# Attention scores as three float32r products of split queries and keys, in a fused attention and feed-forward kernel

## The chip, the core and the metric

The kernel runs on one core of a Trainium2 chip. The core has five engines that work beside each other, each in the order of its own queue: TensorE (PE, matrix products), VectorE (DVE), ScalarE (ACT), GpSimd (POOL) and SyncE (SP, which here only issues transfers). They meet through semaphores. Products land in PSUM, eight banks of 2 KB a partition; all else lives in SBUF, 128 partitions. The metric is the device time of one execution in microseconds, lower being better.

## What is computed

```python
def _attn_ref(q, k, v, tau):                 # (8, 8, 576, 64): batch, heads, positions, width
    scores = matmul(q, k.transpose(0, 1, 3, 2)) / sqrt(64)
    thresh = max(scores, axis=-1, keepdims=True) - tau
    scores = where(scores >= thresh, scores, -1e9)
    scores = scores - max(scores, axis=-1, keepdims=True)
    attn = exp(scores)
    attn = attn / (sum(attn, axis=-1, keepdims=True) + 1e-9)
    return matmul(attn, v)

def _moe_ref(x, w_in, w_out, a, b):          # x: (4608, 512); w_in: (512, 2048)
    h = x @ w_in
    P = a[0] + a[1] * h + a[2] * h**2 + a[3] * h**3
    Q = 1.0 + abs(b[0]) * abs(h) + abs(b[1]) * h**2
    return (P / (Q + 1e-6)) @ w_out
```

The threshold lies only tau = 0.02 below the largest score of a row, so a score that is a little off can fall on the other side of it. That is why the scores are computed to nearly full float32.

## The kernel before

**Tiling.** Heads go in pairs, 4 pairs in each of 8 batches, so 32 pairs. The 576 positions of a pair are cut into four tiles of 128 and a remainder of 64; the remainders of the pair's two heads are put together into one tile. A *unit* is one tile of one pair: 128 full units (two heads each) and 32 remainders. Units are grouped in 56 *visits*, seven a batch: three pairs are visited twice, first for tiles 0 and 1, later for tiles 2, 3 and the remainder, and the fourth pair once, for all of them. Each visit loads the queries that it needs and the keys of its pair.

**A unit.** `f_qk` computes the scores of 128 queries with all 576 keys in float32, each head on its own 64 rows of the array, in a 512-wide and a 64-wide product, into three banks (line 810; line 800 for a remainder). DVE takes the row maximum (818), ACT or DVE the threshold (825, 827), ACT cuts (833) and exponentiates with the sum (837), ACT or DVE the reciprocal's input (842, 844), then the weights are split into two f16 parts (`hi` at 347 or 349, the rest at 859), transposed by DMA from SP (869) and multiplied with the values on PE (928). In the first batch the weights are transposed on PE instead (882, 887) and multiplied in float32 (912).

**The feed-forward part.** It runs in steps of 512 hidden columns for 256 positions: the first layer in three f16 products of parts (1045), the rational function on DVE and ACT (1054 to 1087), the result split in two float32r parts (339 or 341, 1095), the second layer in three float32r products (1104). The weights come as pairs of words; ACT and DVE rebuild the float from them early in the program (`decode_ops`: `f1` 506, `f2` 509, `f4` 513, `f6` 354).

**What sets the order.** The code records operations with engine, duration, sort key, what they follow and which buffers they take and drop. `Plan.order` then walks through a model of the engines and puts each operation into the queue of an engine; operations with two engines in their price table (`FLEX`) go where they would end sooner, weighed by `EARLY` and `PRICE`. `TURN` and `KIND` are tables of numbers that shift the sort keys by place and by kind of operation. An engine's queue runs strictly in the order so made. Where the model sees PE idle in the first 400 us it puts in small products whose result nobody reads (`f_warm`, line 1248).

**The names that the change touches.** `QQs` and `KKs` are two buffers each for queries and keys, float32, loaded from SP by `ldq` and `ldk` inside `load_ops` (lines 643 to 663). `f_qk` reads them directly. In `decode_ops`, `f2` shifts the low words on ACT, and `ld` makes GpSimd wait for an older weight load by a one-element operation (498) where loads would crowd.

Of the kernel before, what the change touches and what calls it, by code (L numbers as in the profile page):

```python
# [46 lines left out]
NQ = 2  # L47
# [93 lines left out]
class Plan:  # L141
# [51 lines left out]
    def order(self):  # L193
# [1097 lines left out]
```

## Time and profile before

| | us |
|---|---|
| median of 2 runs | 1269.24 (1267.21 to 1271.28) |
| the profiled execution | 1266.8 |
| its span, first to last instruction | 1265.0 |
| granted TensorE clock, mean | 0.991 |
| score products on PE (lines 810 and 800), busy | 175.5 + 38.8 |
| second-layer products (1104), busy | 449.1 |
| first-layer products (1045), busy | 403.7 |

A line of a group reads: source line, engine, operation, what it writes and reads, shapes, count, then busy time and the mean duration of one in ns, then the engine's idle time just before such instructions and which instruction ended most of it. Matmul durations reach from a product's start to its drained end, so neighbours overlap and the mean is more than what a product costs in a stream; DVE and ACT records overlap by some tens of ns too, and the busy time counts an overlapped stretch once. A line of a window reads: from, to, length, then busy time and count for PE, PE's weight loads, DVE, ACT and POOL, then the clock, the DMA engines' share and GB/s. A line of waits reads: who waited, for what, us in total, how often, the longest. In the chain and in the timeline the first two numbers are start and length in us.

### The profile page before, as it was taken

Reading aid. Unit: us, or ns where it says so; the run is one execution under the profiler, and the core shown is the slowest. Engines: PE = TensorE matmul, PEld = TensorE weight load, DVE = VectorE, ACT = ScalarE, POOL = GpSimd, SP = SyncE. Lnnn points to the kernel's source line nnn. Section 1 sums busy time; section 2 is a strip of 40 time slices with the busy share of each in tenths; the row PEclk is TensorE's granted clock in tenths of the full one; section 3 lists DMA queues with packets and bytes.
Section 4 is the critical chain, followed back from the end, with each engine's and each line's share of the span. In section 5 each row is a group of like instructions: output and inputs, shape, how many; then the busy total and the mean of one; then the engine's idle time right before and its main releaser. Section 6 shows DMA issues by size and latency. Waiting matters only on the chain. (4 is left out here: it accounts for less than half of the span.)

```text
span 1265.0 us, 25738 instructions
## 1 busy us (share of the span) xinstructions
PE 1226.9 (97%) x9650; PEld 961.6 (76%) x9650; DVE 1188.0 (94%) x1830; ACT 1118.3 (88%) x2185; POOL 97.8 (8%) x217
## 2 busy tenths in 40 slices
PE   8899999999999999999999999999999989999998
PEld 6677777777777777767777777777777767778886
DVE  6999899999999999999999899999999979998787
ACT  7999999999989899988898999899999979895564
POOL 4110000010001100101001100021001100000000
PEclk9999999999999999999999999999999989999999
DMA  6454644675556654665664666667456664542000
GB/s 193 136 167 129 149 81 85 134 151 119 114 95 146 126 110 102 124 121 89 124 116 80 131 125 96 122 120 139 90 112 125 132 109 88 116 88 45 18 17 17
DMA packets 338603, 138.54 MB, mean 110 GB/s; under 512 B 312624, under 2 KB 321712, under 8 KB 338480
## 3 DMA queue, kind: packets, MB, share of 16 engines
q1 hardware_dynamic: 326656, 103.40, 43.9%
q0 software_dynamic: 11072, 32.91, 8.9%
q8 instruction: 76, 1.25, 0.4%
q10 hardware_dynamic: 752, 0.59, 0.2%
q14 instruction: 47, 0.39, 0.1%
HBM read 52.17 MB, written 9.44 MB: 49 GB/s over the span
## 5 line engine op out<-in xcount | busy, mean ns | idle before, releaser
L1104 PE MATMUL banks<-wp,g 128*128 128x512 f32 x1728 | 449.1, 408 | 3.2 <-DVE g L1095 1.7
L1104 PEld LDWEIGHTS banks<-wp,g 128*128 128x128 f32 x1728 | 317.1, 191 | 82.6 <-DVE g L1095 4.4
L1045 PEld LDWEIGHTS <-wi 128*128 128x128 f16 x3456 | 328.8, 98 | 65.3 <-issue 23.3
L1045 PE MATMUL banks<-x,wi 128*128 128x256 f16 x3072 | 360.4, 274 | 3.8 <-ACT t L1054 3.3
L837 ACT ACTIVATE e<-e,cf 128x576 f32<-128x576 f32 x288 | 222.3, 779 | 0.2
L859 DVE SCALAR_TENSOR_TENSOR e<-e,st,hi 128x576 f16<-128x576 f32 x252 | 204.3, 811 | 7.2 <-ACT hi L347 6.5
L833 ACT ACTIVATE e<-banks,st 128x576 f32<-128x576 f32 x288 | 207.2, 739 | 4.2 <-DMA pT<-e 1.9
L347 ACT ACTIVATE hi<-e,st 128x576 f16<-128x576 f32 x225 | 171.0, 770 | 30.2 <-DVE st L848 25.3
L810 PE MATMUL banks<-KK,QQ 64*128 64x64 f32 (+1 forms) x1024 | 175.5, 455 | 7.4 <-ACT e L833 4.5
L818 DVE TENSOR_REDUCE st<-banks 128x2 f32<-128x1152 f32 x128 | 172.3, 1346 | 8.0 <-PE banks L810 7.2
L810 PEld LDWEIGHTS banks<-KK,QQ 64*128 64x128 f32 x1024 | 115.1, 188 | 77.0 <-issue 46.9
L1054 ACT ACTIVATE t<-banks,hsc 128x512 f32<-128x512 f32 (+1 forms) x192 | 106.6, 577 | 26.0 <-PE banks L1045 16.4
L928 PE MATMUL banks<-pT,V 128*64 128x256 f16 (+1 forms) x2520 | 121.7, 250 | 2.6 <-DVE xr L944 2.4
L928 PEld LDWEIGHTS <-V 128*64 128x64 f16 x2520 | 103.7, 111 | 23.3 <-issue 18.8
L1081 DVE SCALAR_TENSOR_TENSOR t<-t,co,t 128x1024 f32<-128x1024 f32 (+1 forms) x73 | 92.2, 1263 | 18.7 <-ACT t L1075 18.6
L1072 ACT ACTIVATE t<-t,co 128x1024 f32<-128x1024 f32 (+1 forms) x73 | 82.9, 1136 | 28.3 <-DVE t L1078 27.0
L1095 DVE TENSOR_TENSOR g<-t,g 128x512 fp32r<-128x512 f32 x144 | 95.2, 683 | 0.8 <-ACT g L339 0.7
L1087 DVE SCALAR_TENSOR_TENSOR t<-t,co,t 128x1024 f32<-128x1024 f32 (+1 forms) x73 | 92.2, 1264 | 0.6
L1065 DVE SCALAR_TENSOR_TENSOR t<-t,co 128x1024 f32<-128x1024 f32 (+1 forms) x73 | 92.2, 1263 | 0.3 <-ACT t L1054 0.3
L1068 DVE SCALAR_TENSOR_TENSOR t<-t,co 128x1024 f32<-128x1024 f32 (+1 forms) x73 | 92.2, 1263 | 0.0
L1078 DVE SCALAR_TENSOR_TENSOR t<-t,co,t 128x1024 f32<-128x1024 f32 (+1 forms) x73 | 92.2, 1263 | 0.0
L1084 DVE SCALAR_TENSOR_TENSOR t<-t,t 128x1024 f32<-128x1024 f32 (+1 forms) x73 | 87.9, 1204 | 0.5
(116 smaller groups left out, 1183.5 us busy)
## 6 DMA issues: line engine op xcount, KB each, us to landing
KK<-in_kT_dram SPq DMA_DIRECT2D x108, 144.0 KB, 3.0
t<-in_w_in_dram POOLq DMA_DIRECT2D x16, 512.0 KB, 4.9
t<-in_w_out_dram POOLq DMA_DIRECT2D x16, 512.0 KB, 4.8
V<-in_v_dram POOLq DMA_DIRECT2D x28, 256.0 KB, 4.4
out_dram<-u POOLq DMA_DIRECT2D x26, 256.0 KB, 3.0
QQ<-in_qT_dram SPq DMA_DIRECT2D x72, 64.0 KB, 2.3
pT<-hi SPq DMA_TRANSPOSE x140, 3.3
pT<-e SPq DMA_TRANSPOSE x140, 3.3
```

The lines of the kernel that those rows point to most:

```text
L347: nc.scalar.activation(dst, src, AF.Identity, scale=factor)
L810: mm = nc.tensor.matmul(s[:, d0:d0 + n], QQ[r, t * P:(t + 1) * P], KK[r, k0:k0 + n], **one)
L818: nc.vector.tensor_reduce(box["st"][:, 0:2], box["both"], AX.X, ALU.max, negate=True)
L833: nc.scalar.activation(ev(hh), box["s"][hh], AF.Prelu, scale=SCALE, bias=box["st"][:, 2 + hh:3 + hh], alpha=STEEP)
L837: nc.scalar.activation(e, e, AF.Exp, scale=passes, accum_out=box["st"][:, 4 + hh:5 + hh])
L859: nc.vector.scalar_tensor_tensor(box["lo"][:, c], ev(hh), box["st"][:, 6 + hh:7 + hh], box["hi"][:, c], ALU.mult, ALU.subtract)
L928: nc.tensor.matmul(dst, V[:, c * P + hh * D:c * P + (hh + 1) * D], rhs, start=c == 0 and n == 0, stop=c == NT and n == 2)
L1045: nc.tensor.matmul(d, wi_tile(c, f0 + j, hl), x[:, c, :], start=c == 0 and n == 0, stop=c == NC - 1 and n == 2)
L1054: nc.scalar.activation(box["h3"][:, 2 * k:2 * k + 2, sl], psv[:, :, sl], AF.Identity, scale=hsc[:, b2, g:g + 1])
L1065: nc.vector.scalar_tensor_tensor(box["r"], box["h"], a2, box["h"], ALU.add, ALU.mult)
L1095: nc.vector.tensor_tensor(fr(g[:, 1]), box["r"][:, k * GW:(k + 1) * GW], g[:, 0], ALU.subtract)
L1104: nc.tensor.matmul(acc[tt], fr(g[:, x]), fr(wo[f][y]), start=begins and j == n == 0, stop=ends and j == nb - 1 and n == 2)
```

## The change

**Scores.** The raw queries and keys are loaded into one tile each (`QR`, `KR`). Each is then split: a copy rounded to float32r (`part_of`, on ACT or DVE), and the rest, raw minus copy, also float32r (`rest_of`, on GpSimd; on DVE for the very first unit). `QS` (two buffers, one unit each) and `KS` (one buffer, all keys of the pair) hold both parts. `f_qk` forms part by part, part by rest and rest by part, adding in PSUM: twelve products for a full unit, six for a remainder. Queries are loaded for two tiles at a time (the second time with the remainder).

**Weights.** `f2`, the shift of the low words, moves from ACT to GpSimd, and the one-element wait before crowded loads goes; a pool of `AHEAD` places in the model stands for it.

**Order.** The model prices a change of PE between kinds of product (`TURNS`), GpSimd's hand-over times change, and `TURN`, `KIND`, `EARLY` and `PRICE` are new throughout, so that every engine's queue is laid out anew.

```diff
-NQ = 2
+NQ, NK = 2, 1
-EARLY = {"ACT": 1.6309, "DVE": 3.9296}
+EARLY = {"ACT": 1.5873, "DVE": 3.8735}
-PRICE = {"ACT": 0.9171, "DVE": 2.3360}
+PRICE = {"ACT": 1.1491, "DVE": 3.0184}
 TURN = [
-    -22753, -3751, -27085, -7959, -27620, -11402, -9570, -6508, -9214, -7383, -6968, -3656, -3744, -4154, -5879,
+    -18202, -5058, -10606, -10532, -34744, -11009, -5499, -5405, -16807, -3769, -3454, -2220, -3468, -3172, -3749,
...
+TURNS = 0.093
...
-    QQs = [const.tile([P, S + REM], F32, name=f"QQ{i}") for i in range(NQ)]
-    for t in QQs:
-        nc.gpsimd.memset(t[:, NT * P:], 0.0)
-    KKs = [const.tile([P, S], F32, name=f"KK{i}") for i in range(NQ)]
+    KR = const.tile([P, S], F32, name="KR")
+    QR = const.tile([P, CT + P], F32, name="QR")
+    nc.gpsimd.memset(QR[:, CT:], 0.0)
+    QSs = [const.tile([P, 2, P], F32, name=f"QS{i}") for i in range(NQ)]
+    KSs = [const.tile([P, 2, S], F32, name=f"KS{i}") for i in range(NK)]
...
-            if len(loaded) >= AHEAD and plan.now - loaded[-AHEAD][1] < RECENT:
-                nc.gpsimd.tensor_scalar(cf[0:1, 15:16], loaded[-AHEAD][0][0:1, 0, 1:2].bitcast(F32), 1.0, 1.0, ALU.mult, ALU.mult)
...
-            nc.scalar.activation(box["rw"][:, :, 0], box["rw"][:, :, 0].bitcast(U32), AF.Copy, scale=2.0 ** -29)
+            nc.gpsimd.tensor_scalar(box["rw"][:, :, 0], box["rw"][:, :, 0].bitcast(U32), 2.0 ** -29, 1.0, ALU.mult, ALU.mult)
...
+    def part_of(x, y, n):
+        copy(fr(x[:, 0, 0:n]), y)
+
+    def rest_of(x, y, n):
+        eng = nc.vector if plan.eng == "DVE" else nc.gpsimd
+        eng.tensor_tensor(fr(x[:, 1, 0:n]), y, x[:, 0, 0:n], ALU.subtract)
+
+    def split(key, hold, slots, y, n, load, take, drop, soon):
+        o = op({"ACT": 0.18 + 0.00075 * n, "DVE": 0.1 + 0.00052 * n}, 0, key, lambda: part_of(slots[hold.slot], y(), n), [load], take, drop)
+        e, d = ("DVE", 0.06 + 0.00104 * n) if soon else ("GD", 0.1 + 0.0021 * n)
+        return op(e, d, key + 0.05, lambda: rest_of(slots[hold.slot], y(), n), [o], (), drop)
...
+            qr = Hold("r", 2 * len(part))
+            w = CT + (REM if NT in part else 0)
+            def ldq(part=part, w=w):
+                c0 = part[0] * P
+                queue.dma_start(QR[0:D, 0:w], qT[bb, pr, :, c0:c0 + w])
+                queue.dma_start(QR[D:P, 0:CT], qT[bb, pr, :, S + REM + c0:S + REM + c0 + CT])
...
-            for hh, k0, n, d0 in (0, NT * P, REM, NT * P), (1, 0, NT * P, w - NT * P), (0, 0, NT * P, 0), (1, NT * P, REM, w - S):
-                r = slice(hh * D, (hh + 1) * D)
-                if d0 == w - S:
-
+            def one(hh, rest, i):
+                r, (x, y) = slice(hh * D, (hh + 1) * D), terms[i]
+                k0, n = (NT * P, REM) if rest else (0, NT * P)
+                d0 = k0 if hh == 0 else w - S if rest else w - NT * P
+                return nc.tensor.matmul(s[:, d0:d0 + n], Q[r, x], K[r, y, k0:k0 + n], start=i == 0, stop=i == 2)
+            for step in "r0 m0 r1 r2 M0 m1 M1 m2 M2 - s0 s1 s2".split():
...
-        qk = op("PE", 1.36 if full else 1.12, p, f_qk, need, [sh[0]], [kh, qh] * nh)
+        need = k_done[bp] + [split(p - 0.3, qh, QSs, lambda: QR[:, c0:c0 + P], P, q_load, [qh], [qr], place_of[bp, t] == 0)]
+        qk = op("PE", 0.80 if full else 0.88, p, f_qk, need, [sh[0]], [kh, qh] * nh, mode=1)
```

What the built programs show of it, at three places. First PE, the start of the program: two units' scores with the warming products around them. `KK` and `QQ` are keys and queries before, a row of "x2" stands for two instructions.

```order
L1248 MATMUL banks<-ident 128x128 x7
L810 MATMUL banks<-KK_114,QQ_110 128x64
L810 MATMUL banks<-KK_114,QQ_110 128x512 x2
L810 MATMUL banks<-KK_114,QQ_110 128x64 x2
L810 MATMUL banks<-KK_114,QQ_110 128x512 x2
L810 MATMUL banks<-KK_114,QQ_110 128x64
L1248 MATMUL banks<-ident 128x128 x6
```

The same place after, `KS` and `QS` being the split keys and queries:

```order
L1285 MATMUL banks<-ident 128x128 x9
L841 MATMUL banks<-KS_115,QS_113 128x64
L841 MATMUL banks<-KS_115,QS_113 128x512
L841 MATMUL banks<-KS_115,QS_113 128x64 x2
L841 MATMUL banks<-KS_115,QS_113 128x512 x5
L841 MATMUL banks<-KS_115,QS_113 128x64 x3
L841 MATMUL banks<-KS_115,QS_114 128x64
```

A unit's four products (each of which the chip carries out as two instructions) have become twelve, with the two heads' products taking turns in the row of five.

Second POOL, where the last weight loads stand. Before, only loads and, behind them, stores and value loads (`V`):

```order
L546 DMA t_70<-in_w_in_dram 128x1024
L582 DMA t_71<-in_w_out_dram 128x1024
L582 DMA t_73<-in_w_out_dram 128x1024
L582 DMA t_71<-in_w_out_dram 128x1024
L582 DMA t_69<-in_w_out_dram 128x1024
L1124 DMA out_dram<-u_75 128x512
L1124 DMA out_dram<-u_76 128x512
```

After, the shifts of the low words (L511) and the subtractions (L646) stand between them:

```order
L585 DMA t_71<-in_w_out_dram 128x1024
L646 TENSOR_TENSOR QS_114<-QR,QS_114 128x128
L646 TENSOR_TENSOR KS_115<-KR,KS_115 128x576
L585 DMA t_72<-in_w_out_dram 128x1024
L585 DMA t_69<-in_w_out_dram 128x1024
L511 TENSOR_SCALAR t_71<-t_71 128x512
L646 TENSOR_TENSOR QS_113<-QR,QS_113 128x128
L511 TENSOR_SCALAR t_72<-t_72 128x512
L511 TENSOR_SCALAR t_69<-t_69 128x512
L646 TENSOR_TENSOR KS_115<-KR,KS_115 128x576
```

POOL's queue, which held loads, stores and memsets, now holds 246 operations on wide tiles too, in one line with the loads and stores.

Third ACT, in the middle of the program, where a full unit's softmax (`st`, `e`, `hi`) runs. Before:

```order
L825 ACTIVATE st_88<-st_88,cf 128x2
L833 ACTIVATE e_79<-banks,st_88 128x576 x2
L837 ACTIVATE e_79,st_88<-e_79,cf 128x576 x2
L1054 ACTIVATE t_73<-banks,hsc 128x512
L1059 ACTIVATE t_68<-t_73 128x1024
L347 ACTIVATE hi_81<-e_79,st_88 128x576
```

After, in such a stretch at the change from one visit to the next:

```order
L878 ACTIVATE st_89<-st_89 128x2
L344 CAST QS_113<-QR 128x128
L344 CAST KS_115<-KR 128x576
L352 ACTIVATE hi_80<-e_79,st_89 128x576
L861 ACTIVATE st_90<-st_90,cf 128x1
L352 ACTIVATE hi_80<-e_79,st_89 128x576
```

The copies of queries and keys stand between a unit's own operations, ahead of its `hi`. Of 160 query copies ACT has 135 and DVE 25, of 56 key copies ACT 50 and DVE 6. In exchange DVE takes 55 casts of g (`t` to `g`) instead of 33 and 19 absolute values instead of 9, with ACT taking that many fewer.

More of the change, by code (lines that the diff above doesn't have):

```diff
@@ L141 @@
 class Plan:
-    LAT = {"PE": 0.27, "ACT": 0.28, "DVE": 0.22, "POOL": 0.16, "DMA": 2.3, "GD": 2.7}
-    OWN = {"PE": 0.0, "ACT": 0.15, "DVE": 0.13, "POOL": 0.1, "DMA": 2.3, "GD": 2.7}
+    LAT = {"PE": 0.27, "ACT": 0.28, "DVE": 0.22, "POOL": 0.16, "DMA": 2.3, "GD": 0.2}
+    OWN = {"PE": 0.0, "ACT": 0.15, "DVE": 0.13, "POOL": 0.1, "DMA": 2.3, "GD": 0.1}
     TO = {("ACT", "DVE"): 0.23, ("ACT", "POOL"): 0.24, ("DVE", "ACT"): 0.2, ("DVE", "PE"): 0.3}
@@ L212, in order @@
         done, busy = [], dict.fromkeys(engines, 0.0)
-        left, wire = len(self.ops), 0.0
+        left, wire, mode = len(self.ops), 0.0, 0
         while left:
@@ L243, in order @@
             o.eng, o.dur = e, o.engs[e]
+            if e == "PE":
+                o.dur += TURNS if o.mode != mode else 0.0
+                mode = o.mode
             for x in o.engs:
@@ L326, in masked_attention_rational_ffn @@
     op = plan.op
-    for name, n in [*POOLS.items(), ("q", NQ), ("k", NQ), ("v", NV)]:
+    for name, n in [*POOLS.items(), ("r", 1), ("kr", 1), ("q", NQ), ("k", NK), ("v", NV), ("w", AHEAD)]:
         plan.pool(name, n)
@@ L521, in f6 @@
                 tensor_tensor(dst.bitcast(I32), t, box["rw"][:, :, 0], ALU.add)
-        l = op("GD", 2.5, key - 2.0, ld, (), [hold], wire=(1.9, 2.0))
+        wh = Hold("w", 1)
+        l = op("GD", 0.65, key - 2.0, ld, (), [hold, wh], wire=(1.9, 2.3))
         if i < NC:
@@ L526, in decode_ops @@
         o1 = op("ACT", 0.567, key, f1, [l], [ht])
-        o2 = op("ACT", 0.568, key, f2, [l])
+        o2 = op("GD", 0.87, key, f2, [l], (), [wh])
         o4 = op("DVE", 0.335, key, f4, [o1])
@@ L633, in masked_attention_rational_ffn, with uses @@
     pairs = {}
+    def uses(ts):
+        return sum(2 if t < NT else 1 for t in ts)
+    def part_of(x, y, n):
[7 more added lines that the diff above has]
+        return op(e, d, key + 0.05, lambda: rest_of(slots[hold.slot], y(), n), [o], (), drop)
     def load_ops(bp, ts):
@@ L637, in load_ops @@
         p = pos[(bp, ts[0])]
-        plan.begin(p - 3.0)
-        n = sum(2 if t < NT else 1 for t in ts)
-        kh, qh = kq[bp] = Hold("k", n), Hold("q", n)
+        plan.begin(p - (3.0 if p else 30.0))
         first = p == 0
@@ L644, in load_ops @@
         queue, eng = (nc.sync, "DMA") if bp < EARLY_QK else (nc.gpsimd, "GD")
-        def ldq():
-            QQ = QQs[qh.slot]
-            c0, c1 = min(ts) * P, min((max(ts) + 1) * P, NT * P)
-            queue.dma_start(QQ[0:D, c0:S if NT in ts else c1], qT[bb, pr, :, c0:S if NT in ts else c1])
-            queue.dma_start(QQ[D:P, c0:c1], qT[bb, pr, :, S + REM + c0:S + REM + c1])
-            if NT in ts:
-                queue.dma_start(QQ[D:P, S:], qT[bb, pr, :, S:S + REM])
+        parts = [x for x in ([t for t in ts if t < NT // 2], [t for t in ts if t >= NT // 2]) if x]
+        raw = Hold("kr", 2)
+        raws.append(raw)
+        kh = kq[bp] = Hold("k", uses(ts))
         def ldk():
@@ L661, in load_ops @@
         issue = {"DMA": 1.25, "GD": 1.1}[eng]
-        q_done[bp] = [op(eng, issue + (0.6 if NT in ts else 0.0), p0, ldq, (), [qh], wire=(0.75 if len(ts) > 3 else 0.4, 1.0))]
-        k_done[bp] = [op(eng, 0.1 if act else issue, p0 + 0.1, ldk, (), [kh], wire=(0.75, 1.0))]
+        for i, part in enumerate(parts):
+            qr = Hold("r", 2 * len(part))
[4 more added lines that the diff above has]
+                queue.dma_start(QR[D:P, 0:CT], qT[bb, pr, :, S + REM + c0:S + REM + c0 + CT])
+                if NT in part:
+                    queue.dma_start(QR[D:P, CT + REM:], qT[bb, pr, :, S:S + REM])
+            key = pos[(bp, part[0])] - 4.0 if i else p0
+            l = op(eng, issue + (0.6 if NT in part else 0.0), key, ldq, (), [qr], wire=(0.5 if NT in part else 0.4, 1.0))
+            kq_loads.append(l)
+            q_of.update({(bp, t): (l, qr) for t in part})
+            if not i:
+                l = op(eng, 0.1 if act else issue, p0 + 0.1, ldk, (), [raw], wire=(0.75, 1.0))
+                k_done[bp] = [split(p - 0.5, kh, KSs, lambda: KR[:, 0:S], S, l, [kh], [raw], first)]
+                kq_loads.append(l)
     place_of = {u: i for i, u in enumerate(units)}
@@ L772, in unit_ops @@
         heads = (0, 1) if full else (0,)
-        kh, qh = kq[bp]
+        kh, qh = kq[bp], Hold("q", 2 if full else 1)
+        q_load, qr = q_of[bp, t]
         plain = is_plain(bp, t)
@@ L790, in f_qk @@
         def f_qk():
-            QQ, KK = QQs[qh.slot], KKs[kh.slot]
+            Q, K = fr(QSs[qh.slot]), fr(KSs[kh.slot])
             h = sh[0]
@@ L794, in f_qk @@
             w = len(h.bank) * 512
-            one = dict(start=True, stop=True)
+            terms = (0, 0), (0, 1), (1, 0)
             if not full:
@@ L799, in f_qk @@
                 for c0, n in (0, NT * P), (NT * P, REM):
-                    nc.tensor.matmul(s[:, c0:c0 + n], QQ[:, NT * P:], KK[:, c0:c0 + n], **one)
+                    for i, (x, y) in enumerate(terms):
+                        nc.tensor.matmul(s[:, c0:c0 + n], Q[:, x], K[:, y, c0:c0 + n], start=i == 0, stop=i == 2)
                 return
@@ L997, in unit_ops @@
         if plain:
-            av = op("PE", 2.36 if full else 0.76, p + 1.2, f_avp, two["tp"] + [v_loaded[bp], x_first.get(ck)], [bh] + first, [two["pT"], vh_[bp]])
+            av = op("PE", 2.175 if full else 0.575, p + 1.2, f_avp, two["tp"] + [v_loaded[bp], x_first.get(ck)], [bh] + first, [two["pT"], vh_[bp]], mode=2)
             plain_av.setdefault(bp, []).append(av)
         else:
-            av = op("PE", 1.86 if full else 0.69, p + 1.2, f_av, two["tp"] + [v_low(bp), x_first.get(ck)], [bh] + first, [two["pT"], vh_[bp]])
+            av = op("PE", 1.675 if full else 0.505, p + 1.2, f_av, two["tp"] + [v_low(bp), x_first.get(ck)], [bh] + first, [two["pT"], vh_[bp]], mode=2)
         x_first.setdefault(ck, av)
```

25 lines of the change are left out of this document (14 added, 11 removed), and 50 rows, old and new, of tables (KIND, TURN).

## The prediction

> **What bounds the kernel now.** I read the page's busy shares first, then the busy time by stage (0 to 50 us: start; 50 to 1156.6: attention with the feed-forward steps; then the last feed-forward steps alone), then the chain of waits, then the groups by form.
>
> ```profile
> PE 1226.9 (97%) x9650; PEld 961.6 (76%) x9650; DVE 1188.0 (94%) x1830; ACT 1118.3 (88%) x2185; POOL 97.8 (8%) x217
> ...
> 0.00:50.00 50.00, 43.13 (x282) 33.84 (x282) 38.69 (x106) 41.85 (x95) 17.74 (x44) 0.97 0.65 188
> 50.00:1156.60 1106.60, 1080.35 (x8721) 843.12 (x8721) 1064.26 (x1636) 1019.04 (x1999) 80.06 (x174) 0.99 0.58 115
> 1156.60:1265.00 108.40, 103.40 (x650) 84.63 (x648) 85.00 (x89) 57.41 (x94) 0.00 (x0) 0.99 0.05 15
> ```
>
> The columns of the stage rows are PE, PE's weight loads, DVE, ACT, POOL. In the long stage PE is idle for 26.3 us of 1106.6 and DVE for 42.3: two engines fill it, and ACT (87.6 idle) is not far. The time is what the tightest engine needs plus the idle that the hand-overs leave. The chain of waits in a piece of this stage runs along PE:
>
> ```profile
> 1030.68 1.23 PE banks L810 x6
> ...
> 1034.95 1.76 PE banks L928 x30
> ...
> 1050.88 1.03 PE banks L800 x4
> ...
> 1192.85 5.26 PE banks L1045 x48
> 1198.10 5.60 PE banks L1104 x24
> ```
>
> The reader is to see what a PE instruction costs in the stream: a unit's scores 1.23 us, a remainder's 1.03, the product of weights and values 1.76, a 512-wide float32r product 5.60 / 24 = 0.233, a 256-wide f16 one 5.26 / 48 = 0.110. The PE columns of durations overlap one another and aren't used.
>
> **The change part by part.** PE, scores. A full unit was four float32 products, each recorded as two instructions (eight), a remainder two products (four).
>
> ```profile
> 502.98 1.35 PE L810 MATMUL banks<-KK,QQ 64*128 64x64 f32 x8
> 504.26 4.10 PE L1045 MATMUL banks<-x,wi 128*128 128x256 f16 x36
> ```
>
> From start to next start a full unit took 1.28 us. It streams twice the columns of a remainder (1.03 us), so the two heads, each on 64 rows of the array, ran largely beside each other. Now each head has three 512-wide and three 64-wide float32r products. If the heads go on overlapping: 3 x 0.233 = 0.70, three 64-wide ones at a quarter of 0.110 each (0.08), and the 0.25 by which the old full unit was longer than a remainder, 1.03; without that last part 0.78; with no overlap twice 0.78, 1.56. I take 1.00, near the row that shows the overlap: 128 x 0.28 = 36 us saved, ends 128 x 0.50 = +64 and 128 x -0.28 = -36. A remainder becomes about 0.85 for 1.03: 32 x 0.18 = 6 us, ends 0 and 8. Together PE frees 42 us. The 33 more warming products (66 instructions) stand where PE would wait, as the others do, and count for nothing; if PE were late there, at 0.110 each they are 7 us.
>
> DVE and ACT. The built order gives the counts; the prices are these rows.
>
> ```profile
> L339 ACT CAST g<-t 128x512 fp32r<-128x512 f32 x111 | 65.3, 612 | 9.6 <-DVE t L1087 9.4
> L341 DVE CAST g<-t 128x512 fp32r<-128x512 f32 x33 | 13.3, 426 | 0.2
> L1059 ACT ACTIVATE t<-t 128x1024 f32<-128x1024 f32 x62 | 65.5, 1056 | 0.7
> L1061 DVE TENSOR_SCALAR t<-t 128x1024 int32<-128x1024 int32 x9 | 6.2, 686 | 0.4 <-ACT t L1054 0.4
> L509 ACT ACTIVATE t<-t 128x512 int32<-128x512 uint32 x32 | 22.3, 707 | 0.0
> L339 ACT COPY pT<-banks 128x128 f32<-128x128 f32 x20 | 6.1, 304 | 0.0
> L875 DVE TENSOR_SCALAR u<-ident,st 128x128 f32<-128x128 f32 x36 | 9.8, 279 | 0.2
> L349 DVE TENSOR_SCALAR hi<-e,st 128x576 f16<-128x576 f32 x27 | 14.2, 524 | 0.3
> L844 DVE TENSOR_SCALAR st<-st 128x2 f32<-128x2 f32 x37 | 6.3, 169 | 7.1 <-ACT e L837 7.1
> ```
>
> DVE gains 22 casts of g (22 x 0.426 = 9.4), 10 absolute values (6.9), 25 query copies (128 wide; by the 279 row at most 7.0), 6 key copies (0.426 x 576/512 = 0.48 each, 2.9) and the first two subtractions (about 1); it gives up 5 `hi` (2.6), 15 reciprocal sums (2.5) and a handful of 0.4 to 0.8 us operations, net 3.9. In all +18 us. If the overlap of neighbouring records is taken off (13.3 / 33 = 0.403 for 0.426) it is +14. ACT loses 32 shifts (22.6), 22 casts (13.5) and 10 absolute values (10.6); it gains 135 query copies (by the 304 row 41) and 50 key copies (0.612 x 576/512 = 0.69, 34.4) and some 13 of small ones: +41, from 1118 to about 1159. ACT has 87.6 us idle in the long stage, so this is covered; if that cover goes, DVE waits for ACT instead.
>
> So PE falls by 42 us to about 1185 and DVE rises to 1206: DVE takes PE's place as the tightest engine. What PE's relief is worth is then bounded by DVE's idle time, 42.3 us in the long stage:
>
> ```profile
> DVE st L818 <- PE banks L810: 7.2, 12, 1.9
> DVE st L844 <- ACT e L837: 7.1, 9, 2.2
> DVE e L859 <- ACT hi L347: 6.5, 10, 1.7
> DVE sc L437 <- ACT u L711: 4.0, 1, 4.0
> DVE sc L437 <- ACT t L554: 2.4, 2, 1.8
> ...
> DVE st L820 <- PE banks L800: 1.8, 5, 0.6
> ```
>
> Waits that name the scores are 7.2 + 1.8 = 9, so 10 us is the low end. The high end is 32: all of the 42.3 but some 10 that hang on chains the scores don't feed (L437's 6.4 and smaller ones). Between them I take the middle, 21.
>
> The end. Behind the last product of attention weights and values stand 384 products of the first layer and 246 of the second, before 396 and 252: 12 x 0.110 + 6 x 0.233 = 2.7 us less. Nothing else changes there.
>
> POOL. It gets 159 subtractions of 128, 55 of 576 and 32 shifts of 512. No row shows such an operation; the nearest on POOL are these.
>
> ```profile
> L690 POOL MEMSET V<- 64x64 f32 x48 | 7.0, 145 | 327.5 <-PE banks L928 182.9 <-issue 143.2
> L629 POOL MEMSET V<- 128x128 f32 x4 | 0.6, 204 | 0.0
> masks.py:199 POOL TENSOR_SCALAR_AFFINE_SELECT ident<-ident 128x128 f32<-128x128 f32 x1 | 0.3, 292 | 0.1
> ```
>
> From below, the two memsets give 0.92 ns an element beyond 64: 0.20, 0.62 and 0.56 us. From above, 292 ns scaled by width: 0.29, 1.31 and 1.17. In all 84 to 155 us on an engine that is busy for 98 of 1265; its own time costs nothing. The Trainium skill ("GPSIMD Engine Reference", section Elementwise, side-by-side cycle accounting) has 4497 ns for 2048 elements of two inputs; scaled as an estimate that is 1.26 us for 576 and about 150 us in all, near the upper end.
>
> Whether that time falls on DVE is the open cost. This is what a POOL DMA issue did to a DVE operation:
>
> ```profile
> 1002.32 0.76 POOL L696 DMA_DIRECT2D V<-in_v_dram  x1
> ...
> 1002.57 0.78 DVE L349 TENSOR_SCALAR hi<-e,st 128x576 f16<-128x576 f32 x1
> ...
> 1003.07 1.05 POOL L700 DMA_DIRECT2D V<-in_v_dram  x2
> ...
> 1003.39 0.81 DVE L859 SCALAR_TENSOR_TENSOR e<-e,st,hi 128x576 f16<-128x576 f32 x1
> ```
>
> The one-input L349 ended with the issue beside it and took 0.78 for a mean of 0.524; the two-input L859 took its usual 0.81 beside the next issue. So the two engines can hold each other up, one operation not always the other. The low end is 0; the high end is all of POOL's new time while DVE is in operations with two inputs from SBUF:
>
> ```profile
> L859 DVE SCALAR_TENSOR_TENSOR e<-e,st,hi 128x576 f16<-128x576 f32 x252 | 204.3, 811 | 7.2 <-ACT hi L347 6.5
> L1065 DVE SCALAR_TENSOR_TENSOR t<-t,co 128x1024 f32<-128x1024 f32 (+1 forms) x73 | 92.2, 1263 | 0.3 <-ACT t L1054 0.3
> L1084 DVE SCALAR_TENSOR_TENSOR t<-t,t 128x1024 f32<-128x1024 f32 (+1 forms) x73 | 87.9, 1204 | 0.5
> L1095 DVE TENSOR_TENSOR g<-t,g 128x512 fp32r<-128x512 f32 x144 | 95.2, 683 | 0.8 <-ACT g L339 0.7
> ```
>
> With four more lines at 92.2 (L1068, L1078, L1081, L1087) these are 848 of DVE's 1188 us; 155 x 0.71 = 110. I take 2, near the L859 row, since most of DVE's time is in such operations; the 110 is a rival below. The Trainium skill ("SBUF — State Buffer", section Who interferes with whom) says that a Vector instruction with two SBUF inputs contends with a GpSimd instruction that reads SBUF, and that the later one waits to the end of the earlier; by that rule the term would be near 110, not 2. The trace agrees for L349; no run here shows POOL reading a wide tile.
>
> Queues. SP issues 160 query loads for 144; each waits for POOL to be done with the single raw tile, and transposes stand behind it. Little hangs on a transpose now:
>
> ```profile
> L833 ACT ACTIVATE e<-banks,st 128x576 f32<-128x576 f32 x288 | 207.2, 739 | 4.2 <-DMA pT<-e 1.9
> ```
>
> so I put nothing there; if each of the 64 query pairs came late by 0.1 us, it would add 6. On POOL the subtractions stand in line with value loads and stores that wait for PE or ACT; a late store would hold the next unit's queries. With two query slots and a unit every 1106.6 / 160 = 6.9 us there is cover. The keys have one slot: from the last score of a visit to the first of the next go a copy (0.69 on ACT) and a subtraction (0.62 to 1.31), some 2 to 2.5 us with hand-overs. By the built order, at the costs in the stream above, PE has 0.9 to 13.7 us of other work there, under 2.5 us in 6 of 55 places: nothing, if the order holds. What would be late next is the subtraction.
>
> Sum against the profiled span: 1265.0 + 18 - 21 - 3 + 2 = 1261. The execution took 1266.8, 1.8 more than its span, so 1263; that execution lies 2.4 below the median of 1269.24.
>
> **The rivals.** POOL holds DVE up (the slower side). For it: the L349 row, and a DVE with no slack. Against it: the L859 row, and that a subtraction may slip in beside L818, which reads PSUM. All of it gives 1263 - 2 + 110 = 1371; about a third, with little idle left to absorb it, 1300. It passes 2% from 32 us on, a fifth of POOL's new time.
>
> Scores get no cheaper. A unit has twelve weight loads for eight. If each had to be served alone, the nearest rows are a product of 0.110 with its load (above) and this:
>
> ```profile
> L882 PE MATMUL banks<-u,e 128*128 128x128 f32 x288 | 38.3, 283 | 6.4 <-ACT pT L339 3.4 <-DVE st L827 2.3 <-DVE u L875 0.7
> ```
>
> 38.3 / 288 = 0.133. A unit then takes 1.32 to 1.60 for 1.28: no gain, the 21 us of relief are gone, 1284; at the upper end PE is at 1268 busy with its 38 idle, 1306. Against it: eight loads fitted into the 1.28 without a gap that shows. The Trainium skill ("TensorE: Matmul & The Clock Gate", section LDWEIGHTS) puts a load of 128 columns at 107 ns whatever its rows; for twelve in one line that is the same 1.28.
>
> The key chain is late: 55 changes of visit each losing 0.5 us are 27 us, less what DVE doesn't feel: 1280. It would be on PE before its first score of a visit.
>
> DVE closes up. If DVE is never idle in the long stage, what is left is 11.3 us at the start and 23.4 at the end: 1206 + 34.7 + 1.8 = 1242, less the 2.7 at the end, 1240. For it: PE manages 98% there today. Against it: DVE has 20 to 40 more hand-overs than now.
>
> **How the numbers follow.** DVE in PE's place at no other cost 0.55 (1263, own range 1246 to 1282); POOL holding DVE up 0.21 (1300, 1285 to 1371); scores no cheaper 0.06 (1284); the key chain 0.08 (1280); DVE closing up 0.10 (1240). Two per cent, about what a measurement of this kernel can tell, is 1243.9 to 1294.6. Faster: the last case and 0.02 of the first, 0.12. Slower: 0.16 of the second and 0.03 each of the third and fourth, 0.22. Same: 0.66. The range 1240 to 1306 leaves out about 0.06 below and 0.12 above, the worse half of POOL's case.
>
> **What would show it.** Right: a score unit of 0.9 to 1.1 us in PE's stream, PE near 1190 busy, DVE near 1206 and the engine with least idle, `hi`, `t` and `g` operations of DVE at the means they have now. POOL's rival: those means longer by 5% or more, or DVE gaps ended by POOL. The key chain: PE idle ended by the subtraction on POOL. Wrong altogether: DVE idle in the long stage under 10 us or over 40.

## The result, and the profile after

The changed kernel takes 1341.26 us (1340.28 to 1342.23, 2 runs) against 1269.24 before: a ratio of 1.057, 95% interval 1.049 to 1.065. It is slower by 72 us, where 1263 was predicted and 1306 was the upper end. The profiled execution spans 1338.5 us, before 1265.0. First the busy shares of the kernel after:

```profile
PE 1251.9 (94%) x10292; PEld 1019.8 (76%) x10292; DVE 1262.7 (94%) x1866; ACT 1149.0 (86%) x2337; POOL 326.5 (24%) x455
```

DVE's busy time rose by 1262.7 - 1188.0 = 74.7 us and the span by 73.5, so DVE's idle time is what it was (75.8 for 77.0). PE, which was to lose 42 us, is at 1251.9, 25 us more. Most of that is its clock. The page's clock row gives the granted clock of PE in 40 equal slices of the span, in tenths of full speed (9 is 90% or more); first the kernel before, then the kernel after:

```profile
PEclk9999999999999999999999999999999989999999
PEclk8889989999999998989999998999899999999999
```

The mean is 0.991 before and 0.971 after. The clock records of the two traces have PE at half speed for 22.6 us before and 77.6 us after, in stretches of 3.4 to 10.2 us (one at the very end is cut shorter); a 512-wide float32r product (L1104, now L1141) there takes 0.427 us from start to next start instead of 0.234. PE is busy for 19.3 us of these stretches before and 65.5 after, and half of the difference is 23 us. In both kernels PE was busy for at most 0.57 of the 3.4 us ahead of each of these stretches (those of the first 10 us aside), so the slow stretches come behind stretches of waiting. What they are worth in time no run here separates from the waiting itself.

By stage (columns as before: PE, weight loads, DVE, ACT, POOL):

```profile
0.00:50.00 50.00, 37.41 (x247) 32.15 (x247) 34.99 (x97) 34.47 (x77) 26.41 (x50) 0.83 0.53 152
50.00:1231.80 1181.80, 1113.32 (x9412) 905.22 (x9412) 1146.90 (x1685) 1058.18 (x2168) 300.05 (x405) 0.98 0.53 109
1231.80:1338.50 106.70, 101.18 (x648) 82.39 (x640) 80.76 (x86) 56.32 (x94) 0.00 (x0) 0.99 0.05 16
```

The loss lies in the long stage: 1181.8 us for 1106.6. The first window is cut at 50 us, so a late start counts into this stage too (DVE did 3.7 us less in the first 50). The end is 1.7 us shorter. Now the groups of DVE and POOL, some that both kernels have and the new ones:

```profile
L895 DVE SCALAR_TENSOR_TENSOR e<-e,st,hi 128x576 f16<-128x576 f32 x252 | 220.2, 874 | 3.0 <-ACT hi L352 2.5
L854 DVE TENSOR_REDUCE st<-banks 128x2 f32<-128x1152 f32 x128 | 172.2, 1346 | 15.4 <-PE banks L841 14.4
L646 POOL TENSOR_TENSOR QS<-QR,QS 128x128 fp32r<-128x128 f32 x159 | 112.7, 709 | 566.1 <-ACT QS L344 478.4
L646 POOL TENSOR_TENSOR KS<-KR,KS 128x576 fp32r<-128x576 f32 x55 | 92.8, 1687 | 126.0 <-ACT KS L344 104.6
...
L346 DVE CAST g<-t 128x512 fp32r<-128x512 f32 x55 | 26.5, 498 | 0.1
L511 POOL TENSOR_SCALAR t<-t 128x512 int32<-128x512 uint32 x32 | 25.5, 797 | 11.8 <-DMA t<-in_w_out_dram 5.3 <-DMA t<-in_w_in_dram 4.6
```

L895, L859 before, now takes 874 ns instead of 811, and the cast of g 498 instead of 426. The row maximum L854, whose input is in PSUM, has kept its mean. If every operation of DVE that both kernels have is compared with its own mean of before, the longer means add up to 58.9 us; operations that are new on DVE (copies, two subtractions) are 10.1 us, and those that came from ACT, less those that went there, 7.1.

The timeline shows how an operation gets longer:

```profile
614.37 0.68 POOL L646 TENSOR_TENSOR QS<-QR,QS 128x128 fp32r<-128x128 f32 x1
614.65 0.68 DVE L346 CAST g<-t 128x512 fp32r<-128x512 f32 x1
...
615.01 1.59 POOL L646 TENSOR_TENSOR KS<-KR,KS 128x576 fp32r<-128x576 f32 x1
...
615.25 1.96 DVE L895 SCALAR_TENSOR_TENSOR e<-e,st,hi 128x576 f16<-128x576 f32 x1
...
616.65 1.17 PE L841 MATMUL banks<-KS,QS 64*128 64x64 f32 x10 [0.64 <-POOL KS L646]
```

The subtraction of the keys ends at 616.60; L895, begun at 615.25, ends 0.61 us after that, having taken 1.96 us for the 0.81 of before. The cast beside the subtraction of the queries takes 0.68. Elsewhere, beside a row maximum, the same subtraction is short and neither is held:

```profile
574.86 0.46 POOL L646 TENSOR_TENSOR QS<-QR,QS 128x128 fp32r<-128x128 f32 x1 [3.70 <-ACT QS L344]
574.90 1.33 DVE L854 TENSOR_REDUCE st<-banks 128x2 f32<-128x1152 f32 x1
```

Last, what the scores cost in PE's stream, a remainder and a full unit:

```profile
565.78 1.22 PE L831 MATMUL banks<-KS,QS 128*128 128x512 f32 x6
566.84 1.42 PE L1141 MATMUL banks<-wp,g 128*128 128x512 f32 x5
...
573.09 1.29 PE L841 MATMUL banks<-KS,QS 64*128 64x64 f32 x12
574.32 1.90 PE L1141 MATMUL banks<-wp,g 128*128 128x512 f32 x7
```

From start to next start, 1.06 us for the remainder (before 1.03) and 1.23 for the full unit (before 1.28). The median of the 128 full units is 1.227, of the 32 remainders 1.036. The scores free PE by about 6 us, not 42.

### The profile page after: what moved, and what is told of

Same layout as the page of the kernel before. It is cut to its first block, busy times and chain, and to the rows that moved or that the text cites. A ratio compares the mean times of both kernels' runs of the same rounds, so it can differ in the third digit from the quotient of the medians.

```text
span 1338.5 us, 27812 instructions
## 1 busy us (share of the span) xinstructions
PE 1251.9 (94%) x10292; PEld 1019.8 (76%) x10292; DVE 1262.7 (94%) x1866; ACT 1149.0 (86%) x2337; POOL 326.5 (24%) x455
## 4 chain that ended last, share of the span: by engine, by line
PE 40%; DVE 29%; ACT 8%; issue 7%; DMA 1%; POOL 0%; SPq 0%; ACTq 0%; DVEq 0%; POOLq 0%
PE banks L1141 17%; PE banks L1082 12%; DVE e L895 6%; PE banks L841 5%; PE banks L964 5%; DVE st L854 3%; DVE t L1118 3%; DVE t L1102 2%; DVE g L1132 2%; DVE t L1121 2%; DVE t L1105 2%; ACT e L869 2%; DVE t L1124 2%; DVE t L1115 1%; ACT hi L352 1%
## 5 line engine op out<-in xcount | busy, mean ns | idle before, releaser
L1141 PE MATMUL banks<-wp,g 128*128 128x512 f32 x1728 | 456.8, 411 | 19.9 <-ACT u L1152 10.1
L1141 PEld LDWEIGHTS banks<-wp,g 128*128 128x128 f32 x1728 | 318.0, 192 | 103.2 <-DVE g L1132 14.1
L1082 PE MATMUL banks<-x,wi 128*128 128x256 f16 x3072 | 366.1, 275 | 16.9 <-ACT t L1091 12.6
L646 POOL TENSOR_TENSOR QS<-QR,QS 128x128 fp32r<-128x128 f32 x159 | 112.7, 709 | 566.1 <-ACT QS L344 478.4
L895 DVE SCALAR_TENSOR_TENSOR e<-e,st,hi 128x576 f16<-128x576 f32 x252 | 220.2, 874 | 3.0 <-ACT hi L352 2.5
L352 ACT ACTIVATE hi<-e,st 128x576 f16<-128x576 f32 x230 | 175.9, 769 | 36.3 <-DVE st L884 25.6
L841 PE MATMUL banks<-KS,QS 64*128 64x64 f32 (+1 forms) x1536 | 172.6, 350 | 23.2 <-ACT e L869 16.8
L841 PEld LDWEIGHTS banks<-KS,QS 64*128 64x128 f32 x1536 | 145.9, 191 | 58.6 <-ACT e L869 27.7
L854 DVE TENSOR_REDUCE st<-banks 128x2 f32<-128x1152 f32 x128 | 172.2, 1346 | 15.4 <-PE banks L841 14.4
L646 POOL TENSOR_TENSOR KS<-KR,KS 128x576 fp32r<-128x576 f32 x55 | 92.8, 1687 | 126.0 <-ACT KS L344 104.6
L1118 DVE SCALAR_TENSOR_TENSOR t<-t,co,t 128x1024 f32<-128x1024 f32 (+1 forms) x73 | 92.8, 1271 | 14.1 <-ACT t L1112 13.7
L1102 DVE SCALAR_TENSOR_TENSOR t<-t,co 128x1024 f32<-128x1024 f32 (+1 forms) x73 | 93.9, 1287 | 3.1 <-ACT t L1091 3.1
L1115 DVE SCALAR_TENSOR_TENSOR t<-t,co,t 128x1024 f32<-128x1024 f32 (+1 forms) x73 | 96.7, 1325 | 0.1
L1124 DVE SCALAR_TENSOR_TENSOR t<-t,co,t 128x1024 f32<-128x1024 f32 (+1 forms) x73 | 95.6, 1310 | 0.5
```

The lines of the kernel that those rows point to most:

```text
L352: nc.scalar.activation(dst, src, AF.Identity, scale=factor)
L646: eng.tensor_tensor(fr(x[:, 1, 0:n]), y, x[:, 0, 0:n], ALU.subtract)
L841: return nc.tensor.matmul(s[:, d0:d0 + n], Q[r, x], K[r, y, k0:k0 + n], start=i == 0, stop=i == 2)
L854: nc.vector.tensor_reduce(box["st"][:, 0:2], box["both"], AX.X, ALU.max, negate=True)
L895: nc.vector.scalar_tensor_tensor(box["lo"][:, c], ev(hh), box["st"][:, 6 + hh:7 + hh], box["hi"][:, c], ALU.mult, ALU.subtract)
L1082: nc.tensor.matmul(d, wi_tile(c, f0 + j, hl), x[:, c, :], start=c == 0 and n == 0, stop=c == NC - 1 and n == 2)
```

## The experiments

The trace offers two causes first, POOL's reads and scores that did not get cheaper. But their sum does not explain 72 us in the prediction's terms: the 21 of missing relief and some 37 of hold-up give 1263 + 58 = 1321. Each experiment below leaves the order of every engine's queue as it stands, but for the operations that it replaces, unless it says otherwise. The edits are shown in part; "..." stands for what is left out. The runs of the kernel before had medians of 1261.7 to 1268.5 us beside them; ratios are to those.

**One column subtracted on POOL.**

```
-        eng.tensor_tensor(fr(x[:, 1, 0:n]), y, x[:, 0, 0:n], ALU.subtract)
...
+        nc.gpsimd.tensor_tensor(fr(x[:, 1, 0:1]), y[:, 0:1], x[:, 0, 0:1], ALU.subtract)
+        nc.gpsimd.memset(x[:, 1, 1:n], 0.0)
```

> The changed kernel, but each subtraction on POOL is done for one column only and the other columns of the rest are filled by a memset on POOL, so the rests are zeros (the cross terms of the scores are left out) while every wait, copy, load, product and place in the queues stays. If POOL's reads of wide tiles hold DVE up: the DVE means come back to those before (L895 near 811 ns, stretch of 59 us down to under 12), DVE busy near 1210, time 1275 to 1295. If it is the lateness of the splits, or the new order, that costs: 1325 to 1345, since both stay.

Measured: 1312.17 us, ratio 1.039 (1.029 to 1.049). Groups and waits:

```profile
L898 DVE SCALAR_TENSOR_TENSOR e<-e,st,hi 128x576 f16<-128x576 f32 x252 | 204.5, 812 | 5.2 <-ACT hi L352 4.8
L648 POOL TENSOR_TENSOR QS<-QR,QS 128x1 fp32r<-128x1 f32 x159 | 55.2, 347 | 588.4 <-ACT QS L344 509.3 <-DVE QS L346 53.8 <-DVE x L983 8.2
```

```profile
DVE st L857 <- PE banks L844: 20.4, 34, 2.4
```

The two-input operation is back at 812 ns and DVE's busy time falls by 46 us to 1216.9. The span falls by only 30, because DVE now waits longer: 20.4 us for scores, where the kernel after has 14.4 and the kernel before 7.2. So the reads do hold DVE up, but a good part of the loss is elsewhere, and the expectation was too low.

**The kernel before, with subtractions, and with memsets, on POOL, that nobody waits for.** There are 160 of 128 columns and 56 of 512, for 159 of 128 and 55 of 576 in the kernel after; the subtractions read a constant tile.

```
+        nc.gpsimd.tensor_tensor(spare[:, 0:n].rearrange("p (c d) -> p c d", d=64), part, part, ALU.subtract)
...
+        nc.gpsimd.memset(spare[:, 0:n], 0.0)
```

> The kernel before, with 160 subtractions of 128 columns and 56 of 512 columns added on POOL, at the scores of each unit, reading a constant tile and writing a spare one that nobody waits for. If POOL's reads hold DVE up: DVE busy grows by 35 to 60 us and the time is 1300 to 1330, with no other part of the change in it. If not: 1265 to 1275, POOL being busy for 18% of the span.

> The same additions as memsets of the same widths, which read nothing. If it is the reading that holds DVE up: DVE means as before and 1265 to 1277. If any work on POOL does it (its queue, its writes): up to that of the kernel with the added reads.

Measured: 1299.02 us, ratio 1.028 (1.019 to 1.038), with the subtractions; 1266.21, ratio 1.000 (0.998 to 1.002), with the memsets. Their groups, the subtractions first:

```profile
L868 DVE SCALAR_TENSOR_TENSOR e<-e,st,hi 128x576 f16<-128x576 f32 x252 | 216.1, 859 | 9.3 <-ACT hi L347 8.8
L392 POOL TENSOR_TENSOR spare<-ident 128x128 f16<-128x128 f32 x160 | 113.5, 710 | 10.2
L392 POOL TENSOR_TENSOR spare<-ident 128x512 f16<-128x512 f32 x56 | 82.1, 1466 | 4.4
```

```profile
L867 DVE SCALAR_TENSOR_TENSOR e<-e,st,hi 128x576 f16<-128x576 f32 x252 | 204.0, 810 | 5.1 <-ACT hi L347 4.4
L391 POOL MEMSET spare<- 128x128 f16 x160 | 35.1, 219 | 6.9
L391 POOL MEMSET spare<- 128x512 f16 x56 | 30.3, 540 | 3.2
```

This is the hold-up by itself: work that nothing waits for makes the old kernel 2.8% slower if it reads SBUF on POOL, and costs nothing if it only writes. The 195.6 us of subtractions added 43 us to DVE's operations. The memsets are shorter, 65.4 us in all; at the same rate they would have added 14 us, and they added 2.

**Products of even width**, 320 and 256 columns instead of 512 and 64.

```
...
-            for step in "r0 m0 r1 r2 M0 m1 M1 m2 M2 - s0 s1 s2".split():
...
+            pieces = {"a": (0, 0, 320), "b": (0, 320, 256), "c": (1, 0, 256), "d": (1, 256, 320)}
...
+            for step in "b0 d0 b1 d1 b2 d2 a0 a1 - c0 a2 c1 c2".split():
```

> The changed kernel with each 576-wide score product cut 320 + 256 in place of 512 + 64, the same number of products and weight loads. If the 64-wide products cost as much as their weight load (0.1 us) and that is why a unit still takes 1.23 us: a unit falls to 0.85 to 1.0 us. If the twelve loads alone set it: 1.2 us as now. As DVE is what the time hangs on, the time falls little: 1322 to 1340; if PE's scores were what cost the time, below 1305.

Measured: 1337.23 us, ratio 1.059 (1.049 to 1.069). The stream:

```profile
564.88 1.06 PE L831 MATMUL banks<-KS,QS 128*128 128x256 f32 x6
565.78 3.67 PE L1141 MATMUL banks<-wp,g 128*128 128x512 f32 x15
...
572.17 1.29 PE L841 MATMUL banks<-KS,QS 64*128 64x256 f32 x12
573.40 0.97 PE L1141 MATMUL banks<-wp,g 128*128 128x512 f32 x3
```

A remainder falls from 1.06 to 0.90 us though its columns are as many: there a 64-wide product costs more than its columns. A full unit stays at 1.23 (1.22 in the median), and the time hardly moves. This version does not give the right output, for a reason that stays open; what is read from it is the time of its products alone.

**Two of the three terms** (eight products a unit), all else as after.

```
-            terms = (0, 0), (0, 1), (1, 0)
+            terms = (0, 0), (0, 1)
...
-            for step in "r0 m0 r1 r2 M0 m1 M1 m2 M2 - s0 s1 s2".split():
+            for step in "r0 m0 r1 M0 m1 M1 - s0 s1".split():
```

> The kernel after with the third term of the scores left out (rest by part): eight products for a full unit instead of twelve, four for a remainder instead of six; every engine's queue is otherwise in the same order. If a unit costs its weight loads (1.227 us / 12 = 0.102 each, whatever the width), a unit falls to about 0.82 us and PE is freed by 128 x 0.41 + 32 x 0.3 = 62 us, more than the prediction's 42. Theory (DVE, held up by POOL, is what sets the time, and PE's relief is worth only what DVE waits for scores): 1320 to 1332 us, DVE's busy time stays near 1263. Rival (PE sets the time): 1280 to 1300 us.

Measured: 1341.48 us, ratio 1.059 (1.054 to 1.064), DVE busy 1263.0: no gain at all from scores that are some 49 us cheaper (a unit 0.93 and a remainder 0.70 in the median, for 1.23 and 1.04). PE's busy time fell by only 26 us, to 1225.6: it is at half clock for 120.1 us of the span now (108.0 of them busy) instead of 77.6 (65.5), which costs it 21 us. With POOL's reads in place this relief of PE bought no time; even the 10 to 20 us that I expected were too many. How much of that is DVE held up and how much the slower clock was not separated.

**No wide reads on POOL**: one column as above, and the shifts of the low words put back on ACT.

```
...
-            nc.gpsimd.tensor_scalar(box["rw"][:, :, 0], box["rw"][:, :, 0].bitcast(U32), 2.0 ** -29, 1.0, ALU.mult, ALU.mult)
+            nc.scalar.activation(box["rw"][:, :, 0], box["rw"][:, :, 0].bitcast(U32), AF.Copy, scale=2.0 ** -29)
```

> The kernel after with one column of each rest subtracted on POOL, the other columns set to zero by a memset, and the shift of the weights' low words put on ACT at the same place of the order: POOL reads no wide tile any more; the rests are zero, so the scores are rounded ones. Theory of the port: what was left of DVE's stretch with the one-column kernel (13 us) goes but for the one-column reads themselves (about 3 to 6 us), so 1300 us (1294 to 1306), DVE busy near 1206, and ACT's 22 us more are covered. Rival (the shifts cost nothing, the rest is order and work that moved to DVE): 1310 to 1316 us.

Measured: 1318.63 us, ratio 1.041 (1.035 to 1.048). DVE's operations are at their old means (3 us of stretch in all), its busy time is 1210.0, yet the time did not fall further. What DVE gained, ACT seems to have taken back: the shifts are 22 us on ACT, and DVE waits 8.0 us for `u` of the weights' decoding (L515 on L508), where the one-column kernel has 2.9. My expectation failed; DVE idle stands at 107.7 us.

**Both: no wide reads and two terms.**

> Both edits together: no wide reads on POOL, and eight products for a unit (third term left out). This is the world that the prediction assumed: no hold-up on DVE and PE freed by 40 to 60 us. If the two failed terms are all that was wrong, it comes to 1263 to 1280 us with DVE near 1206 busy. If the new order itself or the added work costs more than the prediction had, it stays at 1285 to 1300 us.

Measured: 1297.22 us, ratio 1.024 (1.019 to 1.030). Busy shares, and PE's stream:

```profile
PE 1202.4 (93%) x9716; PEld 974.1 (75%) x9716; DVE 1204.2 (93%) x1866; ACT 1157.4 (90%) x2369; POOL 231.8 (18%) x637
```

```profile
550.98 0.99 PE L844 MATMUL banks<-KS,QS 64*128 64x64 f32 x8
551.90 4.47 PE L1144 MATMUL banks<-wp,g 128*128 128x512 f32 x18
```

The wait of DVE for scores, in the kernel without wide reads and here:

```profile
DVE st L857 <- PE banks L844: 21.4, 38, 2.2
```

```profile
DVE st L857 <- PE banks L844: 2.8, 5, 1.1
```

With POOL out of the way cheaper scores are worth 1318.63 - 1297.22 = 21.4 us, and 18.6 of them can be seen in this one wait. PE at 1202 and DVE at 1204 are near the prediction's world (1185 and 1206); the scores here are even cheaper than it had them (0.93 for 1.00 a unit), and PE's slower clock (75.7 us at half speed) makes up for that. Still it takes 1297, not 1263.

**All subtractions on DVE.**

```
-        eng = nc.vector if plan.eng == "DVE" else nc.gpsimd
+        eng = nc.vector
```

> The kernel after with all subtractions on DVE instead of POOL, at the same place of the order; the shifts stay on POOL. The two subtractions that DVE has in the kernel after took 283 and 751 ns, so DVE's own work grows by 159 x 0.283 + 55 x 0.751 = 86 us; the stretch of its other operations falls from 59 to some 13. Theory of the port: net +40, 1365 to 1385 us, so POOL was worth about half of what it took off DVE. Rival (hand-overs to and from POOL cost more than the stretch): 1330 to 1345 us.

Measured: 1349.09 us, ratio 1.065 (1.059 to 1.071).

```profile
L646 DVE TENSOR_TENSOR QS<-QR,QS 128x128 fp32r<-128x128 f32 x160 | 45.7, 286 | 1.2 <-ACT QS L344 1.2
L646 DVE TENSOR_TENSOR KS<-KR,KS 128x576 fp32r<-128x576 f32 x56 | 41.9, 748 | 1.3 <-ACT KS L344 1.3
```

DVE does 87.6 us of subtractions itself and is busy for 1274.0, only 11 more than after; its other operations are at their old means. It came out between the two expectations: having POOL do them gains some 8 us in time, no more than the intervals of the two ratios leave open.

**The scores undone, the order kept**: four float32 products from the raw queries and keys, no copies, no subtractions; first with the shifts on POOL, then on ACT.

```
...
-                return nc.tensor.matmul(s[:, d0:d0 + n], Q[r, x], K[r, y, k0:k0 + n], start=i == 0, stop=i == 2)
...
+                mm = nc.tensor.matmul(s[:, d0:d0 + n], QR[r, c0:c0 + P], KR[r, k0:k0 + n], **one)
```

> The kernel after with the scores undone: four float32 products a unit straight from the raw queries and keys (two key tiles and four query tiles, so that loads need not wait), no copies, no subtractions; every engine's queue is otherwise in the order of after, and POOL still shifts the weights' low words. DVE should be busy for about 1188 + 7 (moved casts) + 8 (shifts holding it up) = 1203 us, and ACT 73 us less than in after. Theory A (the copies, subtractions and hand-overs of the split make all of the loss; the new order costs nothing by itself): 1262 to 1282 us. Theory B (the new order itself leaves DVE and PE idle some 30 us more, as the two kernels without wide reads had it): 1290 to 1310 us.

> The same, with the shift of the low words on ACT at its place of the order: nothing of the change is left but the order and the operations that it gave to another engine. Theory A: 1260 to 1280 us. Theory B: 1290 to 1310 us. Against the run with the shifts on POOL it tells what the shifts are worth there: if holding DVE up costs more than ACT gains, this one is 3 to 10 us faster; if ACT sets the pace while the weights are rebuilt, it is slower by about as much.

Measured: 1306.2 us, ratio 1.032 (1.026 to 1.037), and 1310.72, ratio 1.035 (1.030 to 1.041). Busy shares and the wait for scores of the first:

```profile
PE 1240.8 (95%) x9716; PEld 971.6 (75%) x9716; DVE 1205.0 (92%) x1833; ACT 1097.9 (84%) x2152; POOL 123.7 (9%) x244
```

```profile
DVE st L848 <- PE banks L840: 20.3, 35, 2.3
```

Theory B holds. With nothing of the split left, the new order costs 39 to 44 us. "Order" here includes what comes with it: the operations that it moved between engines and the 66 warming instructions. Of the first kernel's 39 us, 17 are busy time of DVE (7 of them moved operations, 4 longer ones, the rest records that overlap less) and 22 idle time. The scores are those of the old kernel, and DVE waits for them 20.3 us where the old order had it wait 7.2; DVE's idle time is 1304.0 - 1205.0 = 99 us, before 77, PE's 63, before 38. The 32 shifts are no loss on POOL: on ACT the time is 4.5 us more, every run of it above every run with POOL.

**One term** (four products), no wide reads.

> The kernel without wide reads on POOL (one column subtracted, shifts on ACT), now with only the first of the three terms of the scores: four products for a full unit. With twelve products it took 1318.6, with eight 1297.2 us. At 0.1 us a product the unit comes to about 0.5 to 0.6 us (0.926 with eight), below the 0.80 that the order was laid out for. If the new order idles only because scores are dearer than it assumes, this takes another 15 to 22 us off: 1275 to 1283 us. If the relief is used up at the assumed price, it stays at 1288 to 1298 us, and what is left over the kernel before is the order's own.

Measured: 1289.9 us, ratio 1.020 (1.016 to 1.025).

```profile
551.72 0.71 PE L844 MATMUL banks<-KS,QS 64*128 64x64 f32 x4
552.35 3.99 PE L1144 MATMUL banks<-wp,g 128*128 128x512 f32 x16
```

A unit now takes 0.63 us (0.64 in the median). From 1.23 to 0.93 us a unit the time fell by 21.4, from 0.93 to 0.64 by another 7.3 (5 by the ratios): the relief runs out somewhere between the two. That fits the 0.80 (and 0.09 for a change of mode) that the model of the order assumes, but three points do not show where; PE's half clock, 102.4 us for 75.7, is another reason for a smaller gain. What is left, 2% over before, is DVE's added work (1204.0 busy for 1188.0, 16 us) and some idle time of it.

**The order laid out by the measured price.**

```
-        qk = op("PE", 0.80 if full else 0.88, p, f_qk, need, [sh[0]], [kh, qh] * nh, mode=1)
+        qk = op("PE", 1.23 if full else 1.04, p, f_qk, need, [sh[0]], [kh, qh] * nh, mode=1)
```

> The kernel after with the order laid out by the measured price of the scores on PE (1.23 us a full unit and 1.04 a remainder in the model, for 0.80 and 0.88); all else, the tables too, as in after. If the wrong price is what makes the order idle, and the tables still fit, some of the 39 us that the order alone cost comes back: 1310 to 1332 us. If the tables were set for the old price, the order only gets worse: 1341 to 1365 us. This one I hold likelier, since the tables are 390 numbers set with that price.

Measured: 1386.09 us, ratio 1.096 (1.090 to 1.102), worse than both expectations. That fits tables of numbers that go with the price that they were set for. Whether tables set anew for 1.23 would do better was not tried, nor whether they would bring it below the kernel before; no version of the changed kernel here beats that one.

## Why the prediction was wrong

Three things add up, and two ways through the experiments give nearly the same shares (differences of the ratios, times 1267 us; by their intervals the order is uncertain by some 7 us and the other two by 11 to 16, so that the middle one can't be told from nothing). With the shifts on ACT: the order alone 1.0353, with the split's copies and hand-overs but no wide reads 1.0412, with the wide reads 1.0567; that is 45, 7 and 20 us. With the shifts on POOL: 1.0315, 1.0388, 1.0567; that is 40, 9 and 23 us. PE's half clock lies in all three and was not priced by itself: half speed takes 11 us of PE's span before, 19 to 22 with the order alone, 28 without wide reads and 39 in the kernel after.

- **"128 x 0.28 = 36 us saved", "I take 1.00".** Failed. A unit costs 1.23. The terms can be read from the three kernels: 0.64, 0.93 and 1.23 us for four, eight and twelve products, so each term costs 0.29 to 0.30 and 0.34 is fixed, where the sum had 0.26 and 0.25. The 512-wide products of the two heads do overlap, as the sum had it (two of them one after the other would be 0.47 a term); the 64-wide ones are dearer than a quarter of 0.110. In the median unit the three 64-wide products at its head and the product behind them start 0.13, 0.11 and 0.10 us apart, and even widths took 0.15 us off a remainder. Not settled is how much of the full unit's price is the loads, since even widths left it at 1.23. PE, put at 1185 busy, is at 1251.9: the scores took off 6 us, the slower clock added some 23, and the warming products, by the prediction's estimate, 7.
- **The relief of 21 us.** Failed, since the cheaper scores were not there. Without POOL's reads, scores cheaper by some 49 us did give 21.4, but that the figure agrees with the prediction's 21 is luck: 18.6 of it came out of a wait for scores of 21.4 us, and the prediction's 21 out of an order in which that wait was 7.2. With POOL's reads they gave nothing.
- **POOL holding DVE up, "I take 2".** Failed. DVE's own operations grew by 58.9 us, and the time by 20 to 23 on account of the wide reads, where the rival had 37; its direct test in the old order gave 33. I had weighed one L859 that was not held beside a DMA issue against the rule; but a DMA issue is not a read of a wide tile, and that row said nothing about one. The Trainium skill ("SBUF — State Buffer", section Who interferes with whom) separates what reads on GpSimd from what only writes, and says that casts in a two-port mode contend too; the two kernels with work on POOL that nothing waits for (1.028 and 1.000) agree, and the casts of g (498 for 426 ns) would, if they run in such a mode, which no trace shows. My 110 was too much for DVE's 58.9, though POOL's reads took 231 us and not 155: part of POOL's time lies beside operations that it does not touch, such as L854.
- **The order at no cost.** This is the largest step that failed, and it is hardly a step in the prediction: the sum started from the span of before, so it took the idle times of the old order as given, and the change could only shorten them. Measured, the order alone costs 40 to 45 us. The new order was laid out by a score price of 0.80. At the real price DVE waits 20 us for scores; with cheaper scores the wait goes (2.8) and so do 21 to 29 us. That the wrong price is why the order idles is supported by this and not shown outright: what cheaper scores give in the old order was not run, and an order laid out by the real price with these tables was worse still (1386). The rival "scores get no cheaper" had this cause, but priced it as a gain that stays away (1284 to 1306), not as an order that comes apart.
- **DVE's work, +18.** Right: 10.1 + 7.1 = 17.2.
- **ACT's +41, covered.** ACT is at 1149.0, +31, and it is not clear of the path: the scores' products on PE waited 16.8 us for `e` of ACT, before 4.5, to free their banks. How much of that is the copies and how much the order was not separated.
- **The end, -3; keys and queues at 0.** Right: 106.7 for 108.4 us at the end, and PE's idle time ended by a subtraction of keys on POOL is 1.6 us in this row (2.8 for PE's weight loads):

```profile
L841 PE MATMUL banks<-KS,QS 64*128 64x64 f32 x768 | 122.9, 266 | 21.3 <-ACT e L869 16.8 <-POOL KS L646 1.6 <-DVE KS L646 1.4
```

Of the signs that the prediction named, the means of `hi`, `t` and `g` operations and the unit in PE's stream both spoke, at once, for two rivals that it had held apart. Their chances were given as those of single cases, and no case had them together. The sign for "wrong altogether" stayed silent: DVE's idle time in the long stage is 34.9 us, since an operation that is held up counts as busy.

## What to carry to other kernels

Where an order is laid out by a table of prices, a change of prices is a change of the order: first ask whether the new price is real (one unit read from a stream beats a sum of parts), and count what the order loses if it isn't, not only what it doesn't gain. Work given to GpSimd is not free for a VectorE that is the bound when it reads SBUF: here 87.6 us of subtractions moved off DVE gained some 8 us, no clear gain, while memsets cost nothing. When two rivals have different mechanisms, give their sum a chance as well.

## What the runs showed of the hardware

- A subtraction on POOL whose operands have one column took 347 ns in the mean. Of the 128-wide ones in the kernel after, the 36 that overlap no DVE operation or a row maximum alone took 0.46 us in the median, the other 123 took 0.67. That would fit POOL waiting for DVE in its turn; it was not tested by itself.
- One-input casts of DVE (float32 to float32r, 512 wide) were held up as well, 498 for 426 ns; the row maximum from PSUM was not, 1346 ns in both kernels.
- A float32 product in full precision, recorded as two instructions, cost about as much here as three float32r products of parts: 1.28 us a unit against 1.23, 1.03 against 1.04 for a remainder.
- Cheaper products can cost PE its clock: with eight products a unit instead of twelve, all else the same, PE was at half speed for 120.1 us instead of 77.6, without POOL's wide reads for 75.7 instead of 55.1, and with four for 102.4.
